# Loading the w_gate and w_up units as two column halves with 512-byte rows

## The chip, the cores and the metric

The kernel runs on one core of a Trainium2 chip. The metric is the device time of one execution in microseconds (us). Most executions of one kernel here lie within 0.3% of its median, the farthest 0.5% away, so differences below 1% are read from several alternating rounds, with a 95% interval.

## The reference

One decode step of an adaptively normalized transformer layer, together with the gradients of all its inputs, for a single token of width D = 1024:

```python
h = _layernorm(x) * (1 + ca) + sa            # ca, sa, ... from silu(c) @ w_mod
x = x + ga * attention(h, k_cache, v_cache, wq, wo)
h = _layernorm(x) * (1 + cb) + sb
g = h @ w_gate                               # w_gate, w_up: [1024, 3584] bf16
u = h @ w_up
x = x + gb * ((sigmoid(g) * u) @ w_down)     # w_down: [3584, 1024] bf16
# outputs: x and the vector-Jacobian product with grad_out for x, k_cache, v_cache,
# wq, wo, w_gate, w_up, w_down, c, w_mod
```

Each weight is read and a gradient of the same size is written. The gradients of the two caches are 64 MB each and zero outside the last 4096 positions, so 120 stores of 1 MB write zeros. 262 MB move in all. The work is almost entirely data movement.

## The kernel before

The feed-forward part runs over seven blocks of FB = 512 columns. A block needs three units of 1 MB: w_down (`wd`), w_up (`wu`) and w_gate (`wg`). They rotate through five slots of 8 KB a partition. A unit of w_up or w_gate is 1024 rows of the weight by 512 columns: 1024 pieces of 1 KB in memory. Each piece is called a *row* below.

```python
def load_wu(n):
    nc.gpsimd.dma_start(out=wu_t[n], in_=wu_view[:, :, n * FB:(n + 1) * FB])

def load_wg(n):
    nc.gpsimd.dma_start(out=wg_t[n], in_=wg_view[:, :, n * FB:(n + 1) * FB])

load_wd(0); load_wu(0); load_wg(0); load_wd(1); load_wu(1)
# ... attention's output projection; zero(Z_WO[i], mm) puts 6 zero stores on POOL's queue
for n in range(NB):                                   # NB = 7
    # gu = w_up/w_gate columns (stride 4) @ h2; then h, dh, du_b, dg_b (cut)
    zero(Z_FFN[5 * n], None, nc.scalar)               # zero stores on ACT's queue
    # ... w_down's gradient is formed in place (cut)
    nc.sync.dma_start(out=wd_dram(out_8, n), in_=wd_t[n])
    load_wg(n + 1)
    # ... w_up's gradient in place (cut)
    nc.gpsimd.dma_start(out=dwu_view[:, :, n * FB:(n + 1) * FB], in_=wu)
    # ... w_gate's gradient in place (cut)
    nc.gpsimd.dma_start(out=dwg_view[:, :, n * FB:(n + 1) * FB], in_=wg)
    load_wu(n + 2); load_wd(n + 2)
```

A gradient overwrites its weight in SBUF, so a load into a slot waits until the store from that slot has landed. The zero stores on ACT's queue fill the DMA engines while the blocks compute.

## Time and profile before

Median 646.59 us (646.42 to 647.03, 3 runs).

| DMA queue | issued by | carries |
|---|---|---|
| q0 | POOL (descriptors by software) | w_up, w_gate, most gradients, 61 zero stores |
| q1 | SP | the other loads, w_down's gradient |
| q10 | ACT | 59 zero stores, all in the blocks |

All three feed the same 16 DMA engines. A view by stretches gives, for each stretch of the execution, the busy time of each engine in us (PE: matmuls of TensorE, PEld: its weight loads, DVE: VectorE, ACT: ScalarE, POOL: GpSimd; SP, below, is SyncE), with instruction counts, and at the end of the line the granted clock of TensorE as a share of full speed, the busy share of the DMA engines and the GB/s moved. This is the stretch before the first block, where the first three units are loaded nearly alone:

```profile
151.00:167.00 16.00, 5.42 (x108) 5.00 (x109) 5.14 (x22) 2.69 (x6) 1.06 (x2) 0.50 1.04 387
```

The DMA engines are busy all the time (1.04; packets overlap a little) and yet move only 387 GB/s, where the good stretches move about 425.

### The profile page before, as it was taken

Reading aid. Unit: us, or ns where it says so; the run is one execution under the profiler, and the core shown is the slowest. Engines: PE = TensorE matmul, PEld = TensorE weight load, DVE = VectorE, ACT = ScalarE, POOL = GpSimd, SP = SyncE. Lnnn points to the kernel's source line nnn. Section 1 sums busy time; section 2 is a strip of 40 time slices with the busy share of each in tenths; the row PEclk is TensorE's granted clock in tenths of the full one; section 3 lists DMA queues with packets and bytes.
Section 4 is the critical chain, followed back from the end, with each engine's and each line's share of the span. In section 5 each row is a group of like instructions: output and inputs, shape, how many; then the busy total and the mean of one; then the engine's idle time right before and its main releaser. Section 6 shows DMA issues by size and latency. Waiting matters only on the chain.

```text
span 643.5 us, 7106 instructions
## 1 busy us (share of the span) xinstructions
PE 149.8 (23%) x2784; PEld 127.3 (20%) x2784; DVE 319.7 (50%) x626; ACT 206.8 (32%) x306; POOL 83.0 (13%) x137
## 2 busy tenths in 40 slices
PE   3122227562302020020201102310680000424300
PEld 2122215462301020010101101210460000423200
DVE  3442005600844518064180914899800079997194
ACT  2000016610531412543024432789670000425800
POOL 2000000040010100102001010212111012212211
PEclk9999999855555555555555555565755555555555
DMA  9999999999999999999999999999999999999996
GB/s 348 421 425 420 421 420 416 402 411 398 410 422 422 420 414 400 410 398 406 413 368 401 409 416 418 394 382 425 422 423 427 423 424 426 428 426 416 425 426 250
DMA packets 43810, 262.63 MB, mean 408 GB/s; under 512 B 4096, under 2 KB 4096, under 8 KB 18432
## 3 DMA queue, kind: packets, MB, share of 16 engines
q0 software_dynamic: 23184, 131.08, 51.5%
q1 hardware_dynamic: 12048, 69.22, 29.0%
q10 hardware_dynamic: 8544, 61.88, 23.8%
q8 instruction: 22, 0.36, 0.2%
q14 instruction: 12, 0.10, 0.0%
HBM read 76.55 MB, written 185.60 MB: 407 GB/s over the span
## 4 chain that ended last, share of the span: by engine, by line
DMA 64%; DVE 14%; ACT 11%; PE 5%; issue 4%; POOL 1%; SPq 0%; POOLq 0%; ACTq 0%; DVEq 0%
DMA out_dram<-arena 26%; DMA arena<-in_B_w_gate_dram 15%; DVE arena L172 7%; DMA arena<-in_w_mod_dram 7%; DMA arena<-in_A_wq_dram 6%; ACT arena L176 5%; DMA arena<-in_A_k_cache_dram 5%; DMA out_dram<-zeros 4%; DVE junk L172 2%; PE tp_kv L346 2%; DVE arena L168 1%; ACT arena L349 1%; ACT arena L234 1%; PE gu_ps L480 1%; ACT du_b L512 1%
## 5 line engine op out<-in xcount | busy, mean ns | idle before, releaser
L172 DVE CUSTOM_DVE_ANT_0 arena<-arena 128x4096 bf16<-128x4096 bf16 (+1 forms) x24 | 80.1, 3352 | 51.3 <-DMA arena<-in_w_mod_dram 51.3
L480 PE MATMUL gu_ps<-h_bf,arena 128*128 128x1 bf16 x448 | 16.8, 172 | 186.2 <-DMA arena<-in_B_w_up_dram 122.1
L155 DVE TENSOR_TENSOR hh<-sg,gu_ps 128x4 f32<-128x4 f32 x7 | 1.1, 158 | 113.8 <-ACT om L485 113.8
L138 POOL DMA_DIRECT2D out_dram<-zeros x61 | 33.7, 557 | 183.1 <-PE q_ps L315 49.5
L480 PEld LDWEIGHTS <-arena 128*128 128x128 bf16 x448 | 16.2, 118 | 187.9 <-issue 138.7
L653 PEld LDWEIGHTS <-arena 8*128 8x128 bf16 x256 | 25.9, 131 | 102.8 <-issue 99.2
L176 ACT ACTIVATE arena<-du_b,h 128x512 bf16<-128x512 bf16 x56 | 35.2, 711 | 33.8 <-DMA arena<-in_B_w_down_dram 31.3
L176 ACT ACTIVATE arena<-dg_b,h 128x512 bf16<-128x512 bf16 x56 | 35.3, 707 | 25.6 <-DMA out_dram<-zeros 12.7
L349 ACT COPY arena<-tp_kv 128x1024 bf16<-128x1024 bf16 x13 | 13.1, 1010 | 89.6 <-PE tp_kv L346 89.6
L657 ACT CAST arena<-ps_kv 128x512 bf16<-128x512 f32 x32 | 16.1, 691 | 75.1 <-DMA out_dram<-arena 75.1
L172 DVE CUSTOM_DVE_ANT_0 junk<-arena,b1k 128x1024 bf16<-128x1024 bf16 x28 | 34.2, 1223 | 8.2 <-DMA arena<-in_B_w_down_dram 7.7
L172 DVE CUSTOM_DVE_ANT_0 arena<-arena,b1k 128x1024 bf16<-128x1024 bf16 x32 | 36.7, 1218 | 0.4 <-ACT b1k L234 0.4
L172 DVE CUSTOM_DVE_ANT_0 arena<-arena,du_b 128x512 bf16<-128x512 bf16 x56 | 34.9, 686 | 3.5 <-ACT du_b L512 3.5
L172 DVE CUSTOM_DVE_ANT_0 arena<-arena,dg_b 128x512 bf16<-128x512 bf16 x56 | 34.8, 684 | 0.0
L653 PE MATMUL ps_kv<-DO_hd,arena 8*128 8x128 bf16 x128 | 15.9, 296 | 75.1 <-ACT arena L657 75.1
L176 ACT ACTIVATE arena<-b1k,o_col 128x1024 bf16<-128x1024 bf16 x32 | 33.4, 1137 | 0.0
L164 DVE COPY arena<-tp_kv 128x1024 bf16<-128x1024 bf16 x19 | 12.9, 690 | 27.3 <-PE tp_kv L346 27.2
L346 PE MATMUL tp_kv<-ident_bf,arena 128*128 128x128 bf16 x256 | 21.3, 246 | 20.7 <-DMA arena<-in_A_k_cache_dram 12.6
L484 ACT ACTIVATE sg<-gu_ps 128x4 f32<-128x4 f32 x7 | 1.2, 174 | 73.6 <-PE gu_ps L480 73.6
L433 POOL DMA_DIRECT2D arena<-in_B_w_up_dram x7 | 6.2, 891 | 131.3 <-DMA out_dram<-arena 102.3
L659 ACT ACTIVATE arena<-ps_kv 128x512 bf16<-128x512 f32 x32 | 16.1, 624 | 21.6 <-DMA out_dram<-arena 21.6
L346 PEld LDWEIGHTS <-arena 128*128 128x128 bf16 x256 | 18.4, 111 | 23.6 <-DMA arena<-in_A_k_cache_dram 13.5
(185 smaller groups left out, 377.5 us busy)
## 6 DMA issues: line engine op xcount, KB each, us to landing
out_dram<-zeros POOLq DMA_DIRECT2D x61, 1024.0 KB, 20.9
out_dram<-zeros ACTq DMA_DIRECT2D x59, 1024.0 KB, 21.4
out_dram<-arena POOLq DMA_DIRECT2D x46, 1024.0 KB, 20.2
arena<-in_A_wq_dram SPq DMA_DIRECT2D x16, 1024.0 KB, 20.7
arena<-in_w_mod_dram SPq DMA_DIRECT2D x8, 1536.0 KB, 30.8
arena<-in_A_wo_dram SPq DMA_DIRECT2D x8, 1024.0 KB, 23.7
arena<-in_w_mod_dram SPq DMA_DIRECT2D x8, 1024.0 KB, 27.3
arena<-in_B_w_down_dram SPq DMA_DIRECT2D x7, 1024.0 KB, 11.8
```

The costliest lines, as they stand in the source:

```text
L138: ins = nc.gpsimd.dma_start(out=zleft.pop(0).bitcast(FP32), in_=zeros8[:, :])
L164: return nc.vector.tensor_copy(out=out, in_=a)
L168: return nc.vector.tensor_scalar(out=out, in0=a, scalar1=s1, scalar2=None, op0=op0)
L172: return nc.vector.tensor_tensor_reduce(out=out, in0=w, in1=b, scale=1.0, scalar=0.0, op0=ALU.mult, op1=ALU.add, accum_out=acc)
L176: return nc.scalar.activation(out=out, in_=b, func=ACT.Copy, scale=col)
L234: last = nc.scalar.copy(out=o, in_=ps[:, :])
L346: nc.tensor.transpose(tp[:, t8 * P:(t8 + 1) * P], src[:, g, t_ * DH:(t_ + 1) * DH], ident_bf[:, :])
L349: last = nc.scalar.copy(out=o, in_=tp[:, :])
L480: nc.tensor.matmul(gu[:, half * 4 + jj:half * 4 + jj + 1], lhsT=w[:, j, jj::4], rhs=h2_bf[:, j:j + 1], start=(j == 0), stop=(j == KD - 1))
L653: nc.tensor.matmul(ps[:, t4 * DH:(t4 + 1) * DH], lhsT=rows[32 * g:32 * g + HG, t_ * P:(t_ + 1) * P], rhs=hd[32 * g:32 * g + HG, :], start= ...
L657: nc.scalar.copy(out=o, in_=ps[:, :])
L659: nc.scalar.activation(out=o, in_=ps[:, :], func=ACT.Copy, scale=float(scale))
```

## The change

Its intent, as far as the diff shows: smaller pieces of each unit. It issues each unit as two transfers, one for each half of the columns. Every row becomes two of 512 bytes.

```diff
     def load_wu(n):
-        nc.gpsimd.dma_start(out=wu_t[n], in_=wu_view[:, :, n * FB:(n + 1) * FB])
+        for h in range(0, FB, 256):
+            nc.gpsimd.dma_start(out=wu_t[n][:, :, h:h + 256], in_=wu_view[:, :, n * FB + h:n * FB + h + 256])
 
     def load_wg(n):
-        nc.gpsimd.dma_start(out=wg_t[n], in_=wg_view[:, :, n * FB:(n + 1) * FB])
+        for h in range(0, FB, 256):
+            nc.gpsimd.dma_start(out=wg_t[n][:, :, h:h + 256], in_=wg_view[:, :, n * FB + h:n * FB + h + 256])
```

## The prediction

> **What bounds the kernel now.** I read the page's slices first, then its queues, then the chain of waits, then the order of POOL's issues in the feed-forward stage, then single stretches of the DMA view.
>
> ```profile
> DMA  9999999999999999999999999999999999999996
> GB/s 348 421 425 420 421 420 416 402 411 398 410 422 422 420 414 400 410 398 406 413 368 401 409 416 418 394 382 425 422 423 427 423 424 426 428 426 416 425 426 250
> DMA packets 43810, 262.63 MB, mean 408 GB/s; under 512 B 4096, under 2 KB 4096, under 8 KB 18432
> ...
> q0 software_dynamic: 23184, 131.08, 51.5%
> q1 hardware_dynamic: 12048, 69.22, 29.0%
> q10 hardware_dynamic: 8544, 61.88, 23.8%
> ```
>
> The 16 DMA engines are busy in every slice but the last. 262.63 MB at the 425 GB/s of the good slices is 618 us of the 643.5 us span. No compute engine is above half. So the bound is DMA work, and a change counts in two ways: it makes the DMA engines work longer for the same bytes, or it makes them run dry.
>
> ```profile
> DMA 64%; DVE 14%; ACT 11%; PE 5%; issue 4%; POOL 1%; SPq 0%; POOLq 0%; ACTq 0%; DVEq 0%
> DMA out_dram<-arena 26%; DMA arena<-in_B_w_gate_dram 15%; DVE arena L172 7%; DMA arena<-in_w_mod_dram 7%; DMA arena<-in_A_wq_dram 6%; ACT arena L176 5%; DMA arena<-in_A_k_cache_dram 5%; DMA out_dram<-zeros 4%; DVE junk L172 2%; PE tp_kv L346 2%; DVE arena L168 1%; ACT arena L349 1%; ACT arena L234 1%; PE gu_ps L480 1%; ACT du_b L512 1%
> ```
>
> The changed w_gate load is 15% of the chain. In the seven blocks of the feed-forward stage (about 165 to 410 us) the chain repeats "store of w_down's gradient, load of w_gate, 7 us of compute". Zero stores on the ACT queue (q10) fill the DMA engines meanwhile. The issue order of one block:
>
> ```profile
> 294.34 0.89 POOL L433 DMA_DIRECT2D arena<-in_B_w_up_dram  x1 [26.93 <-DMA out_dram<-arena]
> 302.39 0.89 POOL L436 DMA_DIRECT2D arena<-in_B_w_gate_dram  x1 [7.17 <-DMA out_dram<-arena]
> 303.27 0.89 POOL L524 DMA_DIRECT2D out_dram<-arena  x1
> 304.15 0.89 POOL L530 DMA_DIRECT2D out_dram<-arena  x1
> ```
>
> w_up, w_gate and the two gradient stores share one queue (q0) in this order. An issue of 1 MB in 1024 rows holds POOL 0.89 us, while the rest of the transfer is asynchronous.
>
> **What the Trainium skill says.** "DMA: Bandwidth & Descriptors", section "SWDGE vs HWDGE vs iDMA": a packet is preferably at most 4096 B and at most 64 descriptors. The trace agrees: 18432 - 4096 = 14336 packets lie between 2 and 8 KB. 4096 of them are wo's 2 KB rows and 1024 are 4 KB rows of w_mod's gradient. The other 9216 carry the 8 MiB of wo's gradient (2 KB rows) and the 28 MiB of feed-forward loads and stores on q0 (1 KB rows): 36 MiB / 9216 = 4096 B. So q0 packs two 2 KB rows or four 1 KB rows into a packet. Section "Why small descriptors are slow": about 3 cycles per packet, which packing amortizes, and 32 B of metadata per descriptor, which it doesn't. In the packet records a 4096 B packet takes 159 to 161 ns at the median whether it has two rows or four, and an 8192 B one 309 ns: about 9 ns fixed plus 27.3 B/ns. No cost per row shows down to 1 KB; no run yet shows 512 B. Section "Specifications": 512 B is the smallest size without a read-modify-write, so 512 B should just escape. Section "Anatomy of one DMA": descriptor generation is "small, variable". One stretch of this trace seems to disagree, and most of my prediction hangs on it:
>
> ```profile
> 334.01 0.89 POOL L433 DMA_DIRECT2D arena<-in_B_w_up_dram  x1 [28.97 <-DMA out_dram<-zeros]
> ...
> 338.37 0.73 ACTq L140 DMA_DIRECT2D out_dram<-zeros  x1
> ...
> 339.30 0.89 POOL L436 DMA_DIRECT2D arena<-in_B_w_gate_dram  x1 [4.40 <-DMA out_dram<-arena]
> ```
> ```profile
> 334.00:340.00 6.00, 0.00 (x0) 0.00 (x0) 2.48 (x6) 4.43 (x8) 1.59 (x2) 0.50 0.88 300
> 340.00:369.00 29.00, 4.42 (x104) 3.98 (x104) 13.73 (x43) 12.97 (x21) 1.96 (x3) 0.50 1.02 414
> ```
>
> Here q10 and q1 had run dry, so a w_up load met nearly idle engines. They then moved 300 GB/s where the next 29 us had 414 (last column). From the packet records: some 360 rows in the 2 us from 338 to 340, 5.5 ns a row, with q0 packets of 300 to 1400 ns in place of 159. The stalls begin 1.8 us after the issue and end at 6.0 us. In two other blocks whose load started a little early, stalls end 6.1 and 6.2 us after the issue; where the first packet came later (4.9 us or more) there are almost none. I read this as descriptors still being written until 6 us after the issue: (6.0 - 0.7) / 1024 = about 5.2 ns a descriptor. That is an estimate from one full and two partial instances.
>
> **The change part by part.**
> 1. Bytes, dependencies and order on all engines stay. Every matmul reads both halves (it strides the columns by 4), so nothing can start after half a unit.
> 2. Issue: 14 more POOL instructions x 0.89 us = 12.5 us of POOL time. POOL is 13% busy and waits 23 to 29 us before each w_up load, so this is hidden but for up to 0.9 us of latency a unit, which I put inside point 4.
> 3. Data movement: 14 units x 256 packets = 3584 packets of 4096 B, now of eight rows. If 512 B rows cost nothing: 0. If each 4096 B takes 5 to 10 ns longer: 3584 x 5 to 10 ns / 16 engines = 1 to 2 us. If they weren't packed at all, 8 x (9 + 18.75) = 222 ns in place of 159: +14 us, and q0 would lose nearly every turn against 8 KB packets of q10.
> 4. Descriptor generation: 2048 rows a unit, 2 x 5.3 = 10.6 us. The pair w_up + w_gate takes about 0.7 + 21.3 = 22.0 us from w_up's issue to its last descriptor. Before, from that issue to w_gate's last packet, the blocks took (by packet records) 19.9, 20.7, 21.1, 17.4 and 20.7 us. So w_gate comes later by 2.1, 1.3, 0.9, 4.6 and 1.3 us, and by 0.4 us in the block where w_gate comes alone: 10.6 us of the chain. The gradient stores behind it move with it.
> 5. What absorbs it: zero stores still queued on q10 at a block's end. The last block had 1.6 MiB left, 3.9 us at 420 GB/s. 10.6 - 3.9 = about 7 us in which DMA engines have nothing to do. Later stages run at 425 GB/s and cannot win it back.
> 6. The start: the first three units are issued from 136.25 us; six halves of 5.3 us end at 169 us, where w_up's second unit had all been moved by 165 us and q0 was the only queue left. Some 4 us of bandwidth is lost there, but it turns into filler for the blocks after it, so I don't add it to point 5.
>
> Sum if generation binds: +7 us from 5, +1 from 3, so +8. If it doesn't: +1 to 3 us. I give the first reading about 70%.
>
> **The rivals.**
> - *Generation is no limit, rows of 512 B are free* (25%): +0 to 3 us. For it: POOL's own record is only 0.89 us for 1024 rows against 0.53 us for 128, and the skill's "small". Against it: the stalls that end at 6 us three times.
> - *Starved packets block the other queues* (15%, within the first reading): a q0 packet waiting for its eight descriptors keeps its engine from q10's packets. In the stretch at 338 us q10 already had 4 MiB queued and hardly moved. Loads would then drag the whole machine below 300 GB/s for 22 us of each block: +20 to 45 us. Against it: q10's first packets come 3.5 to 5 us after the issue under load anyway, which explains most of that stretch.
> - *No packing, or slow HBM reads at 512 B* (10%): +10 to 15 us, more if q0 loses its turns.
> - *Something gets faster*: only if smaller pieces shared the engines better. Nothing can start on half a unit; 1%.
>
> **Range and chances.** Before is 646.59 us. My middle lies between the two main readings, nearer the first: 653 us, +1.0%. 2% is 659.5 us. The estimate is steep in the generation time: 5.0 ns a row gives about +4 us, 6 ns over +20. Range 647 to 668. Faster 0.01, within 2% 0.70, slower 0.29.
>
> **What would show it.** Packets: the count stays near 43810 plus 14 x 16 = 224 completions, with none between 512 B and 2 KB; if "under 2 KB" jumps by 28,000, packing failed (step 3). Step 4 is right if w_gate's last packet comes about 22 us after w_up's issue and q0's packets are long while they load; wrong if it stays at 20 to 21 us. Step 5 is right if new slices under 400 GB/s appear in blocks 3 to 6 and the stages after 440 us keep their length. A stretch near 160 to 170 us at half bandwidth would show step 6. The prediction fails if the generation time per row differs by 15%, or if starved packets block q10.

## The result, and the profile after

651.92 us median (650.33 to 651.96, 3 runs); ratio to before 1.0073 (1.0049 to 1.0097), slower by 0.7%. A ratio here is the mean time of one kernel's fast runs over that of the other's of the same rounds, so it is not quite the ratio of the medians quoted.

The DMA slices and the packet counts of the page after:

```profile
DMA  9999999999999999999999999999999999999995
GB/s 348 425 422 420 423 421 416 401 410 375 394 421 418 415 410 403 397 399 380 414 373 393 415 408 412 398 382 425 423 422 425 423 426 426 427 425 380 426 423 212
DMA packets 44034, 262.63 MB, mean 404 GB/s; under 512 B 4320, under 2 KB 4320, under 8 KB 18656
...
q0 software_dynamic: 23408, 131.08, 51.5%
```

The 224 packets more are all under 512 B: these are the completions of 14 more transfers, 16 each. None lies between 512 B and 2 KB, so q0 still packs 4096 B, now eight rows, into a packet. The engines are as busy as before, and the tenth slice fell from 398 to 375 GB/s. This is the stretch before the first block again, after the change:

```profile
151.00:167.00 16.00, 4.77 (x93) 4.35 (x94) 4.85 (x19) 2.45 (x4) 3.11 (x6) 0.50 1.04 348
```

348 in place of 387 GB/s, with the same busy share of 1.04. POOL's order in the block whose lines the prediction shows (the same loads and stores; "x2" is the two halves):

```profile
298.06 1.76 POOL L434 DMA_DIRECT2D arena<-in_B_w_up_dram  x2 [27.66 <-DMA out_dram<-arena]
305.36 1.75 POOL L438 DMA_DIRECT2D arena<-in_B_w_gate_dram  x2 [5.53 <-DMA out_dram<-arena]
307.10 0.89 POOL L526 DMA_DIRECT2D out_dram<-arena  x1
307.98 0.90 POOL L532 DMA_DIRECT2D out_dram<-arena  x1
```

The issues of a unit took about 0.87 us more, the order is the same, and the block is 3 to 4 us late.

To see *where* it became late, I took from the packet records the moment at which each kernel had moved a given number of bytes, and subtracted that of before (us). The columns on the right are runs described below.

| MB moved | at (before) | change | change again | rows kept | one transfer | start only | blocks only | 256-byte rows |
|---|---|---|---|---|---|---|---|---|
| 60 | 146.4 | 0.0 | 0.3 | 0.2 | 0.0 | 0.0 | -0.1 | 0.0 |
| 68 | 166.8 | 1.6 | 1.8 | 0.1 | 1.6 | 1.5 | -0.2 | 4.7 |
| 100 | 242.9 | 2.0 | 2.1 | 0.0 | 1.8 | 1.5 | 0.3 | 6.5 |
| 120 | 292.8 | 2.4 | 2.5 | 0.0 | 2.3 | 1.6 | 0.7 | 8.2 |
| 140 | 343.7 | 3.4 | 3.9 | 0.6 | 3.6 | 1.5 | 2.1 | 9.7 |
| 164 | 401.4 | 3.9 | 5.3 | 1.2 | 4.6 | 2.6 | 3.6 | 12.9 |
| 236 | 573.8 | 3.7 | 4.9 | 0.6 | 4.4 | 2.1 | 3.6 | 13.2 |
| 260 | 630.6 | 5.2 | 5.3 | 1.1 | 5.9 | 4.0 | 3.5 | 13.3 |

Each column is one execution, so about 1 us in it is noise ("rows kept" took the same time as before). It shows three things. 1.6 us are lost between 60 and 68 MB, which is the stretch just shown. Over the blocks (68 to 164 MB) another 2.3 us are lost in the first profile of the change and 3.5 in the second. After the blocks nothing is won back. The last row also holds a late stall, described under run 1.

### The profile page after: what moved, and what is told of

It reads as the page before. It is cut to its first block, busy times and chain, and to the rows that moved or that the text cites. A ratio compares the mean times of both kernels' runs of the same rounds, so it can differ in the third digit from the quotient of the medians.

```text
span 650.1 us, 7156 instructions
## 1 busy us (share of the span) xinstructions
PE 150.5 (23%) x2784; PEld 128.0 (20%) x2784; DVE 319.8 (49%) x626; ACT 206.8 (32%) x306; POOL 95.1 (15%) x151
## 4 chain that ended last, share of the span: by engine, by line
DMA 64%; DVE 14%; ACT 11%; PE 5%; issue 3%; POOL 1%; SPq 0%; POOLq 0%; ACTq 0%; DVEq 0%
DMA out_dram<-arena 26%; DMA arena<-in_B_w_gate_dram 14%; DVE arena L172 7%; DMA arena<-in_w_mod_dram 7%; DMA out_dram<-zeros 6%; DMA arena<-in_A_wq_dram 6%; ACT arena L176 5%; DMA arena<-in_A_k_cache_dram 5%; DVE junk L172 2%; PE tp_kv L346 2%; DVE arena L168 1%; ACT arena L349 1%; ACT arena L234 1%; PE gu_ps L482 1%; ACT du_b L514 1%
## 5 line engine op out<-in xcount | busy, mean ns | idle before, releaser
L434 POOL DMA_DIRECT2D arena<-in_B_w_up_dram x14 | 12.4, 890 | 137.1 <-DMA out_dram<-arena 132.0
```

Source lines behind the costliest of these rows:

```text
L434: nc.gpsimd.dma_start(out=wu_t[n][:, :, h:h + 256], in_=wu_view[:, :, n * FB + h:n * FB + h + 256])
```

## The experiments

My theory after the result, called *row size* or *row pace*: a DMA engine needs a fixed time for each row, and shorter rows cost more of it. The rivals: *two transfers* (more issues, fewer transfers outstanding) and *descriptor generation* (the prediction's own).

### 1. The change again

No edit.

> The change again, for its size and for a second profile. Theory 'row size' (eight 512-byte rows per packet are slower to move than four 1 KB rows: in the first profile of the change 176 ns against 166 in the blocks and 209 against 179 at the start): ratio 1.005 to 1.010 again, with the same packet times. Theory 'late stall' (the queue of POOL running dry near 592 us is an accident of that profile): the stretch from 591 to 595 us at half bandwidth would be gone here and the span of the profile 1.4 us shorter.

652.03 us (648.78 to 653.08, 6 runs) against 646.87 (11 runs); ratio 1.0070 (1.0048 to 1.0092). The size holds. The late stall, a stretch near 592 us in which POOL's queue runs nearly dry, was there again but shorter: 2 us at 303 GB/s. By the last two rows of the table it costs from nothing to 1.9 us and varies from run to run; run 2, with rows of 1 KB, has one too (266 GB/s from 588 to 590 us).

### 2. Two transfers, rows kept

```diff
-        nc.gpsimd.dma_start(out=wu_t[n], in_=wu_view[:, :, n * FB:(n + 1) * FB])
+        for h in range(0, KD, 4):
+            nc.gpsimd.dma_start(out=wu_t[n][:, h:h + 4, :], in_=wu_view[:, h:h + 4, n * FB:(n + 1) * FB])
```

and likewise for `wg`.

> Also two transfers for each unit, but split by rows of the weight (each half keeps its 1 KB rows), so the number of transfers, issues and completions is that of the change, while rows and descriptors are those of before. Theory 'row size' and theory 'descriptor generation' (that of the prediction): ratio 1.000, 646 to 647 us. Theory 'two transfers' (0.9 us more POOL issue for each unit and fewer transfers outstanding): ratio 1.006 to 1.008, about 651 us.

646.88 us; ratio 0.9996 (0.9983 to 1.0009). Twice as many transfers cost nothing that shows (at most 0.6 us by the interval). POOL's additional issue time is hidden, and the rival *two transfers* falls.

### 3. One transfer, 512-byte rows

```diff
-        nc.gpsimd.dma_start(out=wu_t[n], in_=wu_view[:, :, n * FB:(n + 1) * FB])
+        wt = B_w_up[0:P, n * FB:n * FB + 256]
+        src = bass.AP(tensor=wt.tensor, offset=wt.offset, ap=[[F, P], [59 * F, 16], [1, 256]])
+        nc.gpsimd.dma_start(out=wu_t[n].rearrange("p j (h f) -> p (j h) f", h=2), in_=src)
```

The rows come from wrong places (16 rows at a step of 59 in place of 8 pairs), so the result is wrong.

> One transfer for each unit, but of 2048 rows of 512 bytes (they are read from wrong places of the weight, so the result is wrong on purpose). Number of transfers as before, rows as in the change. Theory 'row size': ratio 1.004 to 1.009, packets of 4096 bytes at 165 ns beside other queues and near 220 ns alone. Theory 'two transfers': ratio 1.000. Theory 'descriptor generation': as 'row size' in time, but with long packets at the beginning of each load and the pair of loads taking 22 us from issue to last packet.

650.84 us; ratio 1.0060 (1.0043 to 1.0078), the cost of the change within the error. The stretch before the first block, in run 2 and then in run 3:

```profile
151.00:167.00 16.00, 5.75 (x114) 5.26 (x115) 5.38 (x22) 2.69 (x6) 2.71 (x6) 0.50 1.04 389
151.00:167.00 16.00, 4.84 (x95) 4.49 (x96) 4.84 (x19) 2.45 (x4) 1.06 (x2) 0.50 1.04 347
```

Runs 2 and 3 together show that row size is the cause and that the number of transfers is not. Run 3 reads other addresses than the change, but its packets take nearly the same times. In the packet records the 4096 B packets of the first three units took 179 ns in the mean before and in run 2, 205 here, and 209 and 208 in the two profiles of the change. In the blocks their median is 159 ns before and in run 2, and 165 here and in the change.

### 4. The loads by themselves

All but the loads was cut, and on the otherwise idle core seven kinds followed one another, one unit and then four in a row, twice over:

```python
if kind == 0:   nc.gpsimd.dma_start(...)      # w_down, 8 KB rows
elif kind == 1: nc.gpsimd.dma_start(...)      # 1 KB rows
elif kind == 2: ...                           # 1 KB rows, two transfers
elif kind == 3: ...                           # 512-byte rows, two transfers
elif kind == 4: ...                           # 256-byte rows, four transfers
elif kind == 5: nc.sync.dma_start(...)        # 1 KB rows, issued by SP
else:           ...                           # 512-byte rows, issued by SP
```

> Loads of 1 MB by themselves on an otherwise idle core, singly and four in a row, one kind after another: 8 KB rows, 1 KB rows, 1 KB rows as two transfers, 512-byte rows as two transfers, 256-byte rows as four, all issued by POOL, then 1 KB and 512-byte rows issued by SP (no output is written, so the result is wrong on purpose). Theory 'descriptor generation' at 5.2 ns a row: a single load of 1 KB rows takes 6 us or more of packets, 512-byte rows 11 us, 256-byte rows 22 us, while SP's 1 KB rows take 3 us; packets are long and irregular. Theory 'row size' (the DMA engines read at a pace per row, from the start stretch of the change about 28 ns for 512 bytes and 46 ns for 1 KB per engine): 1 KB rows about 3 us of packets, 512-byte rows 3.6 us, 256-byte rows near 5 us, regular packets, and POOL and SP alike.

The view by stretches of this run (only DVE and POOL work, then clock, DMA share and GB/s), in the middle of the four-in-a-row sets: 8 KB, 1 KB, 512-byte and 256-byte rows by POOL, then 1 KB and 512-byte rows by SP.

```profile
53.00:59.00 6.00, 0.44 (x6) 1.80 (x2) 1.00 1.00 422
62.00:82.00 20.00, 1.47 (x21) 10.08 (x13) 1.00 1.03 348
87.00:97.00 10.00, 0.55 (x8) 5.75 (x7) 1.00 1.02 289
101.00:109.00 8.00, 0.44 (x6) 5.80 (x7) 1.00 1.03 215
122.00:130.00 8.00, 0.66 (x9) 0.00 (x0) 1.00 1.10 349
131.00:137.00 6.00, 0.44 (x6) 0.51 (x1) 1.00 1.19 294
```

The DMA share is 1.00 and more everywhere, and the rate falls from 422 to 215 GB/s with the row. For one engine (rate / 16) this is 311 ns for a row of 8 KB, 47.1 for 1 KB, 28.3 for 512 bytes and 19.1 for 256 bytes. All four fit

    time of a row = 9.6 ns + bytes / 27.3 B/ns

within 1 ns. SP's rows go at the same pace as POOL's. SP's are not packed: in the SP stretches the DMA view counts every packet under 2 KB, and in POOL's the packets have 4096 B.

```profile
DMA packets 2761, 2.79 MB, mean 349 GB/s; under 512 B 37, under 2 KB 2761, under 8 KB 2761
```
```profile
DMA packets 1843, 6.96 MB, mean 348 GB/s; under 512 B 144, under 2 KB 144, under 8 KB 1843
```

The first is SP's 1 KB stretch and the second POOL's. So neither packing nor the writer of the descriptors seems to set this pace (the two change together here; that they cancel at both row sizes is unlikely). It is a pace per row. Whether the DMA engine itself sets it, or reading short pieces from HBM, or writing them to SBUF, no run separates.

This run also ends the theory of descriptor generation. A single unit of 256-byte rows (4096 descriptors) on the idle core, issued at 29.87 us; the DMA view of the 6.93 us from that issue:

```profile
29.87 3.50 POOL L119 DMA_DIRECT2D t<-in_B_w_gate_dram  x4 [5.38 <-DVE seen L93]
```
```profile
DMA packets 321, 1.06 MB, mean 153 GB/s; under 512 B 64, under 2 KB 64, under 8 KB 320
...
q0 software_dynamic: 320, 1.05, 64.6%
```

The whole megabyte has gone through by then. By packet records the first packet starts 1.6 us after the issue and the last ends after 6.7, so even if descriptors were written from the issue to the last packet, one takes at most 6.7 / 4096 = 1.6 ns, not 5.2. A unit of 512-byte rows ends 5.9 to 6.2 us after its issue, not 11 or more.

### 5 and 6. The first three units alone, and the blocks alone

```diff
 def load_wu(n):
-    nc.gpsimd.dma_start(out=wu_t[n], ...)
+    if n < 2:        # run 6: n >= 2
+        for h in range(0, FB, 256): ...   # halves, as in the change
+    else:
+        nc.gpsimd.dma_start(out=wu_t[n], ...)
```

`load_wg` has the same with n < 1 (run 6: n >= 1).

> 512-byte rows only for the three units that are loaded before the blocks (about 151 to 167 us), where w_up and w_gate are nearly alone on the DMA engines. Theory 'row pace' (a row costs 9.4 ns plus its bytes at 27.4 B/ns, hidden only where packets of another queue come between): 768 packets x 30 ns / 16 engines = 1.4 us, ratio 1.002 to 1.003, about 648.2 us, all of the lag in bytes moved arising before 172 us. Theory 'blocks only' (the start is absorbed as later filler, as the prediction said in its point 6): ratio 1.000.

> 512-byte rows only for the eleven units loaded in the blocks, the first three with 1 KB rows. Theory 'row pace': packets there take 165 ns in place of 159 at the median, and 7 to 10 ns more in the mean: 2816 x 7 to 10 / 16 = 1.2 to 1.8 us, plus what the stretches without zero stores lose and what the chain loses; ratio 1.004 to 1.006, 649.5 to 650.5 us. If the two parts add up, this and the run before make 5.3 us together.

Start only: 648.86 us, ratio 1.0025 (1.0006 to 1.0044), so 1.6 us. Blocks only: 651.11 us, ratio 1.0062 (1.0041 to 1.0083), so 4.0 us. Together 0.87%, against 0.70 to 0.73% for the whole, which agrees within the errors. The start's lag arises where it was expected, before 68 MB, and is not won back: the column "start only" stays at about 1.5 us over the next 72 MB. Blocks only came out just above the ratio expected (1.004 to 1.006).

In the blocks the packets cost less than the blocks lose. The packet times of the loads there, summed and divided by 16 engines, came to 29.28 us before; to 31.00 and 30.46 in the two profiles of the change, and to 29.70 in run 6. That is 0.4 to 1.7 us more, and run 2, with the rows unchanged, had 0.4 more as well. In run 6 the median rose to 165 ns as expected, but the mean only from 166.4 to 168.7 ns, not by 7 to 10. Runs 10 to 12 go after the rest.

### 7 and 8. Zero stores beside the first loads

If another queue's packets hide the row cost, moving the six zero stores behind the first loads to ACT's queue should remove it there. Run 7 does this to the kernel before, run 8 to the change.

```diff
-            zero(Z_WO[h // 4], mm)
+            zero(Z_WO[h // 4], mm, nc.scalar)
...
-    zero(Z_LN, mm)
+    zero(Z_LN, mm, nc.scalar)
```

> The loads as before the change (1 KB rows), but the six zero stores that stand behind them at 141 to 161 us are issued on ACT's queue, so that their 8 KB packets come between those of w_up and w_gate. Theory 'row pace, hidden by other queues': the packets of the first three units take 160 to 165 ns in place of 179, the stretch from 151 to 167 us moves over 410 GB/s in place of about 385, and the time falls by 0.5 to 2 us (ratio 0.997 to 0.999) unless the attention's own loads are held up by the added queue. Rival 'HBM reads are slower than writes': the packets stay at 175 to 180 ns.

> The change with the same six zero stores moved to ACT's queue. Theory 'row pace, hidden by other queues': the packets of the first three units take 165 to 175 ns in place of 208, and the distance to the run before (mix with 1 KB rows) shrinks from 5.3 to 3.5 to 4.5 us. Rival 'HBM reads are slower for short rows': the first units' packets stay near 208 ns and the distance stays at 5 us or more.

The packets did as the theory said. Over all 768 packets of the first three units the mean is 162.0 ns with 1 KB rows (179 before) and 169.6 ns with 512-byte rows (209 in the change). The stretch is at full pace with 1 KB rows, and the bill comes behind it (run 7, by stretches):

```profile
151.00:167.00 16.00, 3.00 (x44) 2.63 (x44) 2.55 (x16) 3.40 (x5) 0.00 (x0) 0.50 1.03 421
```
```profile
176.00:186.00 10.00, 4.27 (x104) 4.05 (x104) 6.51 (x19) 3.21 (x6) 0.00 (x0) 0.50 0.44 173
```

421 GB/s against 387. But the loads now share the engines and land later. The zero stores are used up when the first block computes, and for 10 us the core moves 173 GB/s. So run 7 is slower: 654.82 us, ratio 1.0115. I had warned only of the attention's loads being held up; the empty queue behind was the actual price. Run 8: 658.88 us, ratio 1.0175. The distance between the two is 1.0175 / 1.0115 = 1.0059, or 3.9 us (4.1 by medians), inside the 3.5 to 4.5 expected. The five runs of each, taken in the same rounds, give 3.8 us (3.0 to 4.7), so the rival's 5 us or more lie just outside. Most of the start's 1.6 us is hidden (768 x 7.6 ns / 16 engines = 0.4 us is left), and the cost of the blocks remains.

### 9. 256-byte rows

The change with a step of 128 columns in place of 256: four transfers a unit.

> Each unit as four transfers of 256-byte rows (16 rows in a packet of 4096 bytes). Theory 'row pace' from the loads by themselves (46.8 ns a row of 1 KB, 28.1 of 512 bytes, 18.9 of 256 bytes per engine): the first three units' packets take about 300 ns in place of 179 (768 x 121 / 16 = 5.8 us), those in the blocks 190 to 230 ns in place of 166 (2816 x 24 to 64 / 16 = 4 to 11 us), and the dry stretches get longer; with the same growth over the direct cost as in the change (5.3 for 3 us): ratio 1.02 to 1.05, 660 to 680 us. Theory 'only the number of transfers': four issues of 0.9 us for each unit, ratio below 1.01. Theory 'descriptor generation' of the prediction (5.2 ns a row, 21 us a unit): w_gate 20 us later in each block, ratio above 1.15.

660.81 us; ratio 1.0229 (1.0198 to 1.0259), 14 us by medians. The direction and the size follow the row pace. By the expectation, the prediction's generation time of 5.2 ns would have cost over 15%; w_gate's last packet came at most 3 us later than before the change, not 20. The packets fell short of what was expected: 261 ns in the mean for the first units (about 300 expected) and 174 ns at the median in the blocks (190 to 230 expected).

### 10 and 11. More zero stores in the blocks

ACT's queue ran dry near 334 us before the change, and in the change too. Run 10 moves three zero stores from just behind the blocks into the third, fourth and fifth block of the kernel before; run 11 does so in the change.

```diff
-Z_FFN = [..., 1, 1, 0, 1, 5, 0, 0, 3, 1, 4, 2, 2, 2, 2, 0, ...]
+Z_FFN = [..., 1, 1, 0, 1, 6, 0, 0, 3, 1, 5, 3, 2, 2, 2, 0, ...]
-Z_T0 = 6
+Z_T0 = 3
```

> The kernel before, with three zero stores moved from just after the blocks into the third, fourth and fifth block, so that ACT's queue does not run dry near 334 us. If the dry stretch costs what its bandwidth says (6 us at 300 in place of 415 GB/s, 1.7 us) and nothing later takes it back: 645 us, ratio 0.997 to 0.999. Rival: the longer queue delays the stores and loads of the chain, ratio 1.000 to 1.005.

> The change with the same three zero stores moved. Theory 'the cost beyond the packets comes from dry stretches that get longer': the distance to the run before (fill with 1 KB rows) falls from 5.3 us to 3 to 4 us, the direct cost of the packets. Rival 'the chain of loads and stores is itself longer': the distance stays at 5 us or more.

Run 10: 647.50 us, ratio 1.0012 (0.9996 to 1.0027). At 140 MB it was 1.5 us ahead of the kernel before, and by 156 MB it was 0.8 us behind; probably the filler was then missing elsewhere. No gain. Run 11: 652.64 us, ratio 1.0094 (1.0076 to 1.0112). The distance is 1.0094 / 1.0012 = 1.0082, or 5.3 us (4.4 to 6.3 from the runs of the two), not the 3 to 4 that I expected. So longer dry stretches are not what the blocks lose beyond their packets; that theory falls.

### 12. Loads and zero stores together, nothing else

Run 4's frame with six loads by POOL beside twelve zero stores by ACT:

```python
for k in range(12):
    if k % 2 == 1:
        ...                                   # a unit, rows of 8 KB, 1 KB, 512 or 256 bytes
    nc.scalar.dma_start(out=zview[...], in_=zeros)
```

> Six loads of 1 MB by POOL beside twelve zero stores of 1 MB by ACT and nothing else, for loads of 8 KB, 1 KB, 512-byte and 256-byte rows in turn (the other outputs are not written, so the result is wrong on purpose). It measures what the blocks' mixture costs per row size. Theory 'row pace, hidden by other queues': while both queues are busy the core moves 415 to 425 GB/s with 8 KB and 1 KB rows, 400 to 412 with 512-byte rows (1.5 to 3% less than with 1 KB, from about 414 and 404 in the blocks), 380 to 400 with 256-byte rows; at 2.5% of the some 90 us in which the blocks load, that is about 2 us of the 4 us that the blocks lose. Rival 'the loss in the blocks is all in the chain': 512-byte rows move within 0.5% of 1 KB rows.

By stretches, each row size twice (8 KB, 1 KB, 512 bytes, 256 bytes), while both queues are busy:

```profile
20.00:40.00 20.00, 0.89 (x12) 3.54 (x4) 1.00 1.01 422
165.00:190.00 25.00, 0.00 (x0) 0.09 (x1) 1.00 1.02 429
60.00:78.00 18.00, 0.44 (x6) 2.33 (x3) 1.00 1.01 416
220.00:250.00 30.00, 0.00 (x0) 0.00 (x0) 1.00 1.02 420
80.00:105.00 25.00, 0.00 (x0) 3.73 (x5) 1.00 1.02 411
265.00:300.00 35.00, 0.00 (x0) 3.53 (x4) 1.00 1.02 405
115.00:155.00 40.00, 0.22 (x3) 15.89 (x18) 1.00 1.02 399
310.00:345.00 35.00, 0.00 (x0) 13.08 (x15) 1.00 1.01 378
```

Mixed with zero stores, 1 KB rows reach 416 to 420 GB/s, 512-byte rows 405 to 411. In the same repetition that is 1.2% less (first) and 3.6% less (second), about the 1.5 to 3% expected; the rival's 0.5% is refuted, as far as one execution can do it. Loads alone lose 17% by the same change (348 to 289). Part of the mixed loss sits in the *other* queue's packets: over these stretches the zero stores' 8 KB packets average 314 ns beside 1 KB rows, both times, and 318 and 329 ns beside 512-byte rows. So the loads' own packet times understate the cost. In the blocks the loads take 86 us in all (the sum, over the blocks before, of the times from the first to the last load packet); 1.2 to 3.6% of 86 us is 1.0 to 3.1 us of the 4.0 that the blocks lose.

The kept profiles of the kernel itself agree. This table compares the stretch from 68 to 164 MB with that of the kernel before, from packet records (us; packet times are summed and divided by 16 engines).

| | change | change again | one transfer | blocks only | rows kept |
|---|---|---|---|---|---|
| stretch longer by | 2.3 | 3.5 | 3.0 | 3.7 | 1.1 |
| packets of all queues longer by | 1.9 | 2.6 | 2.4 | 3.0 | 0.6 |
| of these, zero stores | 0.8 | 0.9 | 0.4 | 1.8 | -0.4 |

So most of what the blocks lose is time in packets, and part of it is in packets of queues that the change did not touch. In the first half (68 to 120 MB), where single executions differ least, the change loses 0.9 and 0.7 us and its packets take 1.0 and 0.9 us longer, against -0.1 and 0.0 for "rows kept".

## Why the prediction was right or wrong

The number was right: +5.3 us measured, 653 predicted (+6.4), within the range, and "within 2%" had the best chance. The mechanism behind most of it was wrong, so the close number is luck.

- **Step 1, nothing moves but the loads: right.** Bytes and order are the same.
- **Step 2, the issue is hidden: right.** Run 2 has all the additional issues and a ratio of 0.9996.
- **Step 3, data movement, 1 to 2 us: the right step, mis-sized.** The reading that rests on it alone gave +1 to 3 us, and 5.3 were measured. It was sized with one packet time for all stages, 5 to 10 ns more. The median in the blocks rose by 6 ns, within that. At the start, where few packets of other queues come between, the mean rose by 30 ns: 768 x 30 / 16 = 1.4 us, and run 5 gives 1.6 us in time. In the blocks the loss also falls on the zero stores beside the loads (run 12 and the table under it). The row's fixed time was visible before the change: I derived 9 ns per *packet* from packets beside other queues and concluded that a row costs nothing, while the slow stretch at 151 to 167 us (387 GB/s at a full DMA share) said that rows do cost something when they are alone.
- **Step 4, descriptor generation at 5.2 ns a row, w_gate about 22.0 us behind w_up's issue: wrong.** From w_up's issue to w_gate's last packet the change took 21.0, 21.3, 19.7, 17.4 and 21.0 us, much as before (19.9, 20.7, 21.1, 17.4, 20.7). Run 4 bounds generation at 1.6 ns a descriptor. I had read a stall as the writing of descriptors because it ended 6 us after the issue in three cases. But at this place the long packets end 6.6 and 7.0 us after the issue in the two profiles of the change, with twice the descriptors, and 4.2 us after it in run 9, with four times as many. I also took the queues for dry, while q1 still moved some 280 to 380 GB/s in the first 2 us of that stretch; and zero stores came back at 6 us, which ended the load's demand on idle engines.
- **Step 5, filler absorbs a part: not supported.** Filler added to the blocks left the distance at 5.3 us (runs 10 and 11). The 7 us in which engines have nothing to do are not there: from 68 to 164 MB the time without a packet, averaged over the 16 engines (counted where fewer than 16 packets are open), was 0.8 us before, 1.3 and 1.8 in the change, and 1.3 in "rows kept". The sign that I had named did appear (new slices under 400 GB/s in the blocks, later stages as long as before), so it could not tell this step from slower packets.
- **Step 5, later stages cannot win it back: right.** The lag hardly changes from 164 to 236 MB in any column.
- **Step 6, a loss at the start: right place, wrong account.** I expected 4 us of lost bandwidth that turns into filler and so costs nothing. It is 1.6 us (0.4 to 2.8 by the interval), and it stays to the end (run 5).
- **The rivals.** "Rows of 512 B are free" is refuted by run 3. "No packing": the packet counts refute it. "Starved packets block the other queues" would have cost 20 to 45 us; nothing of that size appeared.

The sum came out close because the term that I gave 70% (+7 us, wrong) stood in for terms that I had sized too low (start, and mixture in the blocks). A right total from a wrong mechanism carries nothing over to another kernel.

What stays open. Of the 4.0 us of the blocks, the mixture of run 12 explains 1.0 to 3.1, and the packet records of the kernel put 1.9 to 3.0 us into packets. The rest is no larger than the spread of single executions ("rows kept" differs by 1.1 us); whether the chain of loads and stores adds to it, no run separates. What makes the first packets of some loads take 300 to 1400 ns is not settled either. In run 4 single loads on an idle core have such packets too: up to 2% of them on SP's queue, about 1 to 5% on POOL's, and also in a unit of 8 KB rows (the longest 1059 ns, 309 at the median), which has only 128 rows. So many descriptors are not needed for it.

## What to carry to other kernels

Look at GB/s beside the DMA busy share: the engines that were full at 387 GB/s, where other stretches reach 425, were paying per row, and shorter rows cost most exactly there. Two short runs separate the number of transfers from the size of rows: split along the dimension that keeps rows whole, and one transfer with short rows. And before trusting a rate read off one odd stretch, measure the suspected part by itself; run 4 would have corrected step 4 of this prediction in one execution.

## What the Trainium skill lacked or had wrong

- "DMA: Bandwidth & Descriptors", "Specifications", gives 512 B as the minimum for line rate. In the loads by themselves 512-byte rows moved 289 GB/s and 1 KB rows 348, against 422 with 8 KB rows, so 512 B was not enough here.
- The same page, "Why small descriptors are slow", says that packetization amortizes the fixed time per packet, and is worth it only at 256 B or less. In run 4 rows packed into 4096 B and unpacked rows move at the same pace (348 and 349 GB/s at 1 KB, 289 and 294 at 512 bytes), which fits the second half; smaller rows were not tried unpacked. The time per row that all sizes show, packed or not, a fixed 9.6 ns, does not stand there.
- That another queue's large packets hide most of this is on none of the pages that I read: 1.2 to 3.6% lost from 1 KB to 512 bytes beside zero stores, 17% without them.
- The same page, "Anatomy of one DMA", calls descriptor generation "small, variable". My reading of one stretch spoke against it, and run 4 agrees with the page: at most 1.6 ns a descriptor for 4096 of them. No figure per descriptor stands in that place; this bound would have prevented the error.
